# Transposing x on row halves into two banks, with fewer zero products and a newly written order of all engines

## The chip, the cores and the metric

The kernel runs on one core of a Trainium2 chip. The metric is the device time of one execution in microseconds; the time before, 137.42 us, is the median of three runs.

## The reference

Sliding-window attention with a linear position bias, and behind it a token-mixing layer whose weights are made from the attention's output. Eight batches, eight heads, 576 tokens, head dimension 64, so a model width of 512.

```python
scores = q @ k.T / sqrt(64) + slope[h] * -(i - j)    # only where 0 <= i - j < 128
attn   = softmax(scores);  x = attn @ v              # per batch and head
x      = x transposed to (batch, token, 512)
W_tok  = (x @ w_q) @ (x @ w_k).T / 8                 # 576 x 576 per batch
out    = relu(W_tok @ x) @ w_out
```

## The kernel before, in words

The work of a batch is cut into named steps, and everything that an engine does stands in one written table, `ORDER` (line 49). An entry such as `XT2.0:P00` gives the step, the engine (P TensorE, A ScalarE, D VectorE, G GpSimd's DMA queue, S SyncE's DMA queue) and for TensorE the PSUM pair and bank: there are four pairs of two banks, one digit names a whole pair, two digits one bank. `follow` (line 145) walks through the table and each step's instructions are issued in that order, so every engine's queue is exactly its column of the table, in order. Semaphores between engines are put in from the data.

The steps of batch b, key block or row block in the second number:
- `LF`, `Lq`, `Lk`, `Lv`, `Lt` load q, k, v and the 64 tail tokens. The first six, `LF`, bring batch 0's first blocks in fp32 through the queues of ScalarE and SyncE, 128 KB each (line 412). All others go through GpSimd's queue and are cast to fp16 on the way.
- `TF`, `TJ`, `TQ`, `TK`, `TT` transpose q and k on TensorE (lines 465 to 608), and `EF`, `EJ`, `ETQ`, `ETK`, `ETT` copy them from PSUM to `qkT`. TK uses the helper `tp2` (line 245): it transposes 64 rows at a time, the upper and the lower half into two different banks of a pair, so 16 small transposes make one step.
- `QK` makes the scores of four heads for 128 keys, `EXP` (line 657) exponentiates them on ScalarE into `pt`, and one `MUL` (line 672) on VectorE multiplies the eight heads of a key block by the tabled exponential of bias and mask.
- `PV` multiplies by v with a column of ones; `RC` takes the reciprocal of the sums and `X` (line 733) scales into `x`, 128 tokens at a time. Part 4 is the tail of 64 tokens.
- `XT` (line 749) transposes two blocks of x: eight transposes of 128 x 128 into one bank. `EXT` copies the result to `xT`. The other branch in the same function, for b >= `PAIRED`, does it with `tp2` into both banks of a pair, sixteen transposes of 64 rows; with `PAIRED = 9` and eight batches it is never taken. `XTT` does the tails.
- For a pair of batches (0 and 1, 2 and 3, ...; steps carry the even number) `WK`, `WQ`, `WT` project with w_k and w_q, `G` makes the 64 x 512 product of keys and x, `MX` the mixed tokens, `RM` and `RMT` the relu, `OUT` the output product of 128 tokens, `EO` the copy to one of 14 buffers `osb` and `DO` the store to memory, through SyncE's queue with two exceptions on ScalarE's.
- `WM` (line 297) issues products of a zeroed tile with itself, whose result nobody reads; `WARM` gives their number at each place of the table.

The work of a pair's mixing and output lies in the table among the scores of the next batches. Only the last pair's has nothing to lie beside.

Of the kernel before, what the change touches and what calls it, by code (L numbers as in the profile page):

```python
# [15 lines left out]
S = 576  # L16
D = 64
# [25 lines left out]
PAIRED = 9  # L43
# [7 lines left out]
zeros:D LF0.1.0.1:S Lv2.4:G ones.1:D Lq0.2:G pads:D Lk0.2:G wmc:D WM.0:P31 TF0.0.0:P00 Lk0.1:G  # L51
ones.3:D bias:A Lq1.0:G ones.0:D TF0.0.1:P01 idh:D Lk1.0:G TF0.1.1:P10 EF0.0.1:D Lk1.1:G
TF0.1.0:P11 EF0.1.1:D Lv0.0:G EF0.0.0:A EF0.1.0:A Lk1.2:G Lk1.3:G WM.1:P31 TJ0.2.1:P1
QK0.0.1:P0 QK0.0.0:P2 EJ0.2.1:D Lv0.1:G TJ0.2.0:P30 EXP0.0.0:A TJ0.1.1:P1 EJ0.2.0:D Lk0.3:G
EXP0.0.1:A QK0.2.1:P3 EJ0.1.1:D QK0.2.0:P2 QK0.1.1:P1 EXP0.2.1:A MUL0.0:D TQ1:P0 EXP0.2.0:A
Lv0.2:G QK0.1.0:P3 Lt0:G ETQ1:D EXP0.1.0:A TK1.0:P2 ETK1.0:D EXP0.1.1:A Lv1.0:G MUL0.2:D
WM.2:P01 QK1.1.1:P2 QK1.1.0:P3 QK1.0.1:P1 EXP1.1.1:A Lv1.1:G QK1.0.0:P0 MUL0.1:D EXP1.1.0:A
Lq2.0:G TK1.1:P2 ETK1.1:D EXP1.0.1:A Lk2.3:G PV0.0:P3 QK1.2.1:P2 RC0.0:D Lk2.2:G X0.0:D
EXP1.0.0:A PV0.1:P1 MUL1.1:D PV0.2:P3 Lv1.2:G EXP1.2.1:A QK1.2.0:P0 Lv0.3:G RC0.1:D EXP1.2.0:A
X0.1:D TT0:P2 RC0.2:D Lv1.3:G TJ0.3.1:P1 X0.2:D ETT0:A XT0.0:P00 ETT1:A MUL1.0:D Lk2.0:G  # L60
EJ0.3.1:A WM.3:P01 QK1.3.0:P2 Lv0.4:G EXP1.3.0:A EXT0.0:D PV1.0:P1 QK0.3.1:P3 RC1.0:D PV1.1:P0
X1.0:D EXP0.3.1:A QK0.3.0:P2 MUL1.2:D QK1.3.1:P1 EXP0.3.0:A TQ2:P3 Lk2.1:G RC1.1:D EXP1.3.1:A
MUL0.3:D Lv1.4:G ETQ2:A WM.4:P21 TK2.1:P1 X1.1:D Lt1:G ETK2.1:D PV1.2:P2 XT1.0:P00 RC1.2:D
PV0.3:P3 X1.2:D Lw1:G QK2.2.1:P1 MUL1.3:D Lk3.1:G EXP2.2.1:A Lw0:G RC0.3:D WM.5:P01 PV1.3:P2
EXT1.0:A X0.3:D Lq3.0:G PV0.4:P01 RC1.3:D X1.3:D TK2.0:P3 QK2.2.0:P1 Lv2.0:G RC0.4:D PV1.4:P00
ETK2.0:D EXP2.2.0:A XT1.1:P20 Lk3.0:G RC1.4:D X0.4:D QK2.0.0:P3 EXT1.1:D XT0.1:P21 EXP2.0.0:A
# [93 lines left out]
def kernel(  # L160
# [914 lines left out]
```

## Time and profile before

| | us |
|---|---|
| median of three runs | 137.42 |
| lowest and highest | 137.33, 138.28 |
| span of the profiled execution, first to last instruction | 135.4 |
| median less span | 2.0 |
| TensorE busy | 122.8 |
| VectorE busy | 114.0 |
| ScalarE busy | 107.3 |
| GpSimd busy (it issues the loads, 0.9 us each) | 86.3 |

The profiled execution's own time is known by its span of 135.4 us; the runs' times are taken around the whole execution, and their median lies 2.0 us above it. Times in views count from the start of the span. A row of a group gives line, engine, operation, destination and sources, shape and count, then the busy time of all, the mean of one in ns, and the idle time of the engine just ahead of them with what ended it. A row of the table of stretches gives the stretch and its length, then busy time (and count) of TensorE, its weight loads (PEld), VectorE, ScalarE and GpSimd, the granted clock, the DMA share and GB/s. Busy times of TensorE overlap, so its share reads high.

### The profile page before, as it was taken

Reading aid. Unit: us, or ns where it says so; the run is one execution under the profiler, and the core shown is the slowest. Engines: PE = TensorE matmul, PEld = TensorE weight load, DVE = VectorE, ACT = ScalarE, POOL = GpSimd, SP = SyncE. Lnnn points to the kernel's source line nnn. Section 1 sums busy time; section 2 is a strip of 40 time slices with the busy share of each in tenths; the row PEclk is TensorE's granted clock in tenths of the full one; section 3 lists DMA queues with packets and bytes.
Section 4 is the critical chain, followed back from the end, with each engine's and each line's share of the span. In section 5 each row is a group of like instructions: output and inputs, shape, how many; then the busy total and the mean of one; then the engine's idle time right before and its main releaser. Section 6 shows DMA issues by size and latency. Waiting matters only on the chain.

```text
span 135.4 us, 5054 instructions
## 1 busy us (share of the span) xinstructions
PE 122.8 (91%) x2174; PEld 78.1 (58%) x2174; DVE 114.0 (84%) x197; ACT 107.3 (79%) x145; POOL 86.3 (64%) x108
## 2 busy tenths in 40 slices
PE   6598867889999799999999999999999999999970
PEld 2264546666676476575566576565685576634440
DVE  5733899999999999998999999699999999557830
ACT  2574999995999999998999999999999962367040
POOL 7998979599979759899999999997000000000000
PEclk9999999999999999999999999999999999999999
DMA  4999999999999999999999999999999900858894
GB/s 106 211 165 169 155 156 180 165 158 154 167 159 163 195 184 153 157 154 157 155 157 158 152 153 155 151 185 258 269 223 348 331 14 5 258 185 328 264 368 151
DMA packets 105414, 24.97 MB, mean 184 GB/s; under 512 B 95536, under 2 KB 100912, under 8 KB 105392
## 3 DMA queue, kind: packets, MB, share of 16 engines
q0 software_dynamic: 96832, 14.42, 150.2%
q1 hardware_dynamic: 6688, 9.44, 20.4%
q10 hardware_dynamic: 1872, 0.79, 2.2%
q8 instruction: 17, 0.28, 0.8%
q14 instruction: 5, 0.04, 0.1%
HBM read 29.62 MB, written 9.44 MB: 288 GB/s over the span
## 4 chain that ended last, share of the span: by engine, by line
PE 67%; DVE 13%; ACT 10%; DMA 3%; issue 3%; ACTq 1%; DVEq 0%
PE pair L240 54%; PE pair L243 12%; ACT pt L657 6%; DVE pt L672 4%; DVE qkT L254 4%; DMA osb<-in_q_dram 3%; DVE x L733 3%; ACT qkT L252 2%; DVE rm L888 1%; ACTq L412 1%; ACT rm L886 1%; DVE inv L723 1%; ACT wqT L252 0%; DVE xT L254 0%; ACT gs L252 0%
## 5 line engine op out<-in xcount | busy, mean ns | idle before, releaser
L657 ACT ACTIVATE pt<-pair 128x1024 f16<-128x1024 f32 x64 | 62.8, 1038 | 6.5 <-PE pair L240 5.9
L672 DVE TENSOR_TENSOR pt<-pt,bias 128x2048 f16<-128x2048 f16 x32 | 38.5, 1217 | 0.4 <-ACT pt L657 0.3
L393 POOL DMA_DIRECT2D vt<-in_v_dram x40 | 35.3, 968 | 1.1 <-issue 0.5
L240 PE MATMUL pair<-wout_sb,rm 128*128 128x512 f16 (+1 forms) x132 | 31.7, 373 | 0.0
L367 POOL DMA_DIRECT2D natk<-in_k_dram x31 | 28.6, 947 | 2.9 <-DMA natq<-in_q_dram 1.6
L240 PE MATMUL pair<-vt,pt 128*128 128x65 f16 (+1 forms) x576 | 21.9, 194 | 1.9 <-DVE rm L888 0.5
L240 PEld LDWEIGHTS <-pt 128*128 128x128 f16 (+1 forms) x576 | 19.1, 100 | 7.6 <-issue 3.4
L240 PE MATMUL pair<-qkT 64*128 64x256 f16 (+2 forms) x320 | 22.3, 250 | 1.3 <-DVE qkT L254 0.8
L254 DVE COPY qkT<-pair 128x1024 f16<-128x1024 f16 (+2 forms) x27 | 19.3, 734 | 4.1 <-PE pair L243 3.9
L733 DVE TENSOR_TENSOR x<-pair,inv 128x512 f16<-128x512 f32 x32 | 21.8, 690 | 0.9
L252 ACT COPY osb<-pair 128x512 f32<-128x512 f32 (+1 forms) x24 | 14.0, 596 | 10.5 <-PE pair L240 9.7
L240 PEld LDWEIGHTS <-rm 128*128 128x128 f16 x132 | 11.4, 97 | 12.1 <-issue 2.2
L240 PEld LDWEIGHTS <-qkT 64*128 64x128 f16 x320 | 11.1, 94 | 8.6 <-issue 5.4
L254 DVE COPY osb<-pair 128x512 f32<-128x512 f32 (+1 forms) x13 | 8.7, 668 | 5.1 <-PE pair L240 5.1
L379 POOL DMA_DIRECT2D natq<-in_q_dram x12 | 11.5, 995 | 2.2 <-PE pair L240 1.6
L886 ACT ACTIVATE rm<-pair 128x1024 f16<-128x1024 f32 x11 | 11.1, 1045 | 0.5 <-PE pair L240 0.3
L243 PE MATMUL pair<-identh,x 128*128 128x128 f16 x128 | 9.8, 220 | 0.0
L240 PE MATMUL pair<-warm 128*128 128x512 f16 x22 | 7.8, 491 | 1.5 <-DVE warm L295 1.2
L243 PEld LDWEIGHTS <-x 128*128 128x128 f16 x128 | 7.6, 98 | 2.3 <-issue 1.2
L254 DVE COPY xT<-pair 128x1024 f16<-128x1024 f16 x11 | 7.5, 685 | 1.2 <-PE pair L243 1.1
L243 PE MATMUL pair<-identh,natk 64*128 64x64 f16 x248 | 6.5, 191 | 1.2 <-ACT pt L657 0.9
L243 PEld LDWEIGHTS <-natk 64*128 64x128 f16 x248 | 5.3, 94 | 3.9 <-issue 3.3
(68 smaller groups left out, 136.2 us busy)
## 6 DMA issues: line engine op xcount, KB each, us to landing
out_dram<-osb SPq DMA_DIRECT2D x30, 256.0 KB, 3.5
vt<-in_v_dram POOLq DMA_DIRECT2D x32, 128.0 KB, 7.2
natk<-in_k_dram POOLq DMA_DIRECT2D x31, 128.0 KB, 5.8
natq<-in_q_dram POOLq DMA_DIRECT2D x4, 512.0 KB, 7.7
natq<-in_q_dram POOLq DMA_DIRECT2D x12, 128.0 KB, 5.7
out_dram<-osb SPq DMA_DIRECT2D x9, 128.0 KB, 2.5
vt<-in_v_dram POOLq DMA_DIRECT2D x8, 64.0 KB, 5.7
natt<-in_q_dram POOLq DMA_DIRECT2D x4, 128.0 KB, 5.7
```

The lines of the kernel that those rows point to most:

```text
L240: hold(nc.tensor.matmul(*a, **k))
L243: hold(nc.tensor.transpose(*a))
L252: hold(nc.scalar.copy(out_ap, in_ap))
L254: hold(nc.vector.tensor_copy(out=out_ap, in_=in_ap))
L367: return lambda: nc.gpsimd.dma_start(out=natk(b, n), in_=k[b, :, P * n:P * n + P, :].transpose([1, 0, 2]))
L379: return lambda: nc.gpsimd.dma_start(out=rows_q(b)[:, r], in_=q[b, :, 0:512, :].rearrange("h (p r) d -> r p h d", r=QR)[r])
L393: return lambda: nc.gpsimd.dma_start(out=vtv(b, t)[:n, :, 0:D], in_=v[b, :, P * t:P * t + n, :].transpose([1, 0, 2]))
L412: (nc.scalar if o.eng == "ACT" else nc.sync).dma_start(out=nat32(j, n)[:, 4 * u:4 * u + 4, :], in_=(q, k)[j][0, 4 * u:4 * u + 4, P * n:P * ...
L657: nc.scalar.activation(out=pt, in_=two(hold_.bank).rearrange("p e c -> p (e c)"), func=AF.Exp, scale=SCALE)
L672: nc.vector.tensor_tensor(out=pv, in0=pv, in1=bt, op=ALU.mult)
L733: nc.vector.tensor_tensor(out=x_s[b % NX][qt].rearrange("p (g h d) -> p g h d", g=2, h=4), in0=sums(p)[:, :, :, 0:64], in1=box["inv"].unsq ...
L886: hold(nc.scalar.activation(out=out_ap, in_=in_ap, func=AF.Relu, scale=WSCALE))
```

## The change

`PAIRED` goes from 9 to 0: every XT now takes 64 rows at a time with `tp2`, the two halves into the two banks of a pair, and EXT reads both. `WARM` goes from 22 zero products at six places to 15 at four: seven ahead of everything, two ahead of the first scores, two between the first scores and the next, four in batch 1. `ORDER` is another table: the same steps (less two WM), but another order on every engine, other engines for many copies, and other banks.

```diff
-PAIRED = 9
+PAIRED = 0
...
-WARM = (6, 9, 1, 1, 2, 3,)
+WARM = (7, 2, 2, 4,)
...
 ORDER = """
-warm:D LF0.0.0.0:A LF0.0.1.0:S ones.2:D iota:G LF0.0.1.1:A LF0.1.0.0:S ident:G LF0.0.0.1:A
...
+warm:D iota:G ones.2:D LF0.0.1.0:S LF0.1.0.0:A WM.0:P31 ident:G LF0.0.0.0:S wmc:D LF0.1.0.1:S
+Lq0.2:G LF0.0.0.1:S Lk0.2:G ones.1:D LF0.0.1.1:S bias:A Lk0.1:G idh:D pads:D TF0.1.0:P00 ones.0:D
```

The engines' queues at three places. First ScalarE at the start of the program; `osb` are the first loads, `bias` the table of the mask, `qkT0` batch 0's transposed q and k, `pt` the exponentials, `pair` a PSUM pair. Before:

```order
L412 DMA osb_145<-in_q_dram 128x4x64
L412 DMA osb_147<-in_k_dram 128x4x64
L412 DMA osb_145<-in_q_dram 128x4x64
L336 ACT_TABLE_LOAD
L336 ACTIVATE bias_71<-wm_70 128x384 x8
L252 CAST qkT0_76<-pair0_140 128x2x2x128
L252 CAST qkT0_76<-pair1_141 128x2x128
L657 ACTIVATE pt0_98<-pair2_142 128x1024
```

Now:

```order
L408 DMA osb_151<-in_q_dram 128x4x64
L332 ACT_TABLE_LOAD
L332 ACTIVATE bias_71<-wm_70 128x384 x8
L248 CAST qkT0_76<-pair1_141 128x2x2x128
L248 CAST qkT0_76<-pair0_140 128x2x2x128
L248 CAST qkT0_76<-pair0_140 128x2x128
L653 ACTIVATE pt0_98<-pair1_141 128x1024
L248 COPY qkT0_76<-pair0_140 128x4x256
L653 ACTIVATE pt0_98<-pair1_141 128x1024
```

Two of its three loads have moved to SyncE's queue; it has one copy of transposed blocks more ahead of its first exponential, and another between the first and the second. (Lines of the changed kernel are four lower.)

SyncE's queue, where the first stores stand. Before, the first three rows behind the loads:

```order
L412 DMA osb_147<-in_k_dram 128x4x64
L412 DMA osb_154<-in_q_dram 128x4x64 x2
L993 DMA out_0_dram<-osb_2048 128x512
L993 DMA out_0_dram<-osb_1219 128x512
L993 DMA out_0_dram<-osb_2022 128x512
```

Now:

```order
L408 DMA osb_149<-in_k_dram 128x4x64
L408 DMA osb_164<-in_q_dram 128x4x64
L408 DMA osb_151<-in_q_dram 128x4x64
L408 DMA osb_164<-in_q_dram 128x4x64
L408 DMA osb_149<-in_k_dram 128x4x64
L989 DMA out_0_dram<-osb_1364 128x512
L989 DMA out_0_dram<-osb_1542 128x512
L989 DMA out_0_dram<-osb_1250 128x512
L992 DMA out_0_dram<-osb_1189 64x512 x2
```

The queue has five first loads where it had three. Its first store was DO3.3, which stands in the table behind the exponentials of batch 6's third block; now it is DO0.1, behind those of batch 3, and five more stores of batches 0 and 1 follow it among the steps of batch 4.

VectorE from its last multiply (`pt`) on; `inv` and `invt` are reciprocals, `x32` a block of x of batch 7, `xtl` tails, `xT` the copied transposes of x, `wqT` and `wkt` projections. Before:

```order
L672 TENSOR_TENSOR pt0_98<-pt0_98,bias_71 128x2048
L888 TENSOR_SCALAR rm0_136<-pair0_140 128x8x4x32
L254 CAST wqT1_129<-pair1_141 128x64
L254 CAST wkt1_133<-pair1_141 64x2x64 x2
L723 RECIPROCAL inv_2634<-pair3_143 128x8
L733 TENSOR_TENSOR x32_118<-pair3_143,inv_2634 128x512
L723 RECIPROCAL inv_2649<-pair2_142 128x8
L723 RECIPROCAL inv_2651<-pair1_141 128x8
L733 TENSOR_TENSOR x33_119<-pair2_142,inv_2649 128x512
L733 TENSOR_TENSOR x30_116<-pair1_141,inv_2651 128x512
L723 RECIPROCAL inv_2679<-pair3_143 128x8
L733 TENSOR_TENSOR x31_117<-pair3_143,inv_2679 128x512
```

Now, from the fifth row behind the last multiply on; ahead of these stand the reciprocals and products of two other blocks of batch 7:

```order
L719 RECIPROCAL inv_2702<-pair0_140 128x8
L729 TENSOR_TENSOR x33_119<-pair0_140,inv_2702 128x512
L719 RECIPROCAL inv_2740<-pair3_143 128x8
L729 TENSOR_TENSOR x23_115<-pair3_143,inv_2740 128x512
L716 RECIPROCAL invt_2792<-pair0_140 128x4
L723 TENSOR_TENSOR xtl1_121<-pair0_140,invt_2792 128x256
L716 RECIPROCAL invt_2812<-pair0_140 128x4
L723 TENSOR_TENSOR xtl1_121<-pair0_140,invt_2812 128x256
L250 COPY xT2_124<-pair3_143 128x2x4x2x64
L250 COPY xTt1_127<-pair1_141 128x512
L250 CAST gs1_135<-pair1_141 128x512
```

A relu and, behind the rows shown, six copies of the output of batches 4 and 5 have left the end of VectorE's queue; blocks of batch 6 that stood ahead of the last multiply (x23 and the tails) now stand behind it, and the copies of xT follow them directly. In TensorE's queue, behind the last scores, 14 output products stand where 19 stood (a product of halves counted as one), and WT6 stands behind WK6, where it stood ahead of the last PV steps.

More of the change, by code (lines that the diff above doesn't have):

```diff
@@ L55 @@
[L55 to L60, printed above, removed]
@@ L115 @@
-OUT6.2:P11 DO7.2:A EO6.0:D OUT6.1:P30 DO6.0:S EO6.2:D OUT6.3:P10 DO6.2:S EO6.1:D OUT7.0:P11
-DO6.1:S EO6.3:D OUT7.1:P30 DO6.3:S EO7.0:A OUT7.3b:P10 DO7.0:S EO7.1:A OUT7.3a:P11 EO7.3b:D
-DO7.1:S DO7.3b:A EO7.3a:A DO7.3a:S
+warm:D iota:G ones.2:D LF0.0.1.0:S LF0.1.0.0:A WM.0:P31 ident:G LF0.0.0.0:S wmc:D LF0.1.0.1:S
+Lq0.2:G LF0.0.0.1:S Lk0.2:G ones.1:D LF0.0.1.1:S bias:A Lk0.1:G idh:D pads:D TF0.1.0:P00 ones.0:D
+Lt0:G TF0.0.0:P01 zeros:D TF0.1.1:P10 TF0.0.1:P11 EF0.1.1:D Lk0.3:G ones.3:D WM.1:P31 Lq1.0:G
```

119 lines of the change are left out of this document (61 added, 58 removed).

## The prediction

> **What bounds the kernel now.** I read the slices of the page first, then the table of stretches, the groups by shape, the order of events at both ends, and the landings of loads.
>
> Busy tenths of TensorE (PE), VectorE (DVE) and ScalarE (ACT) in 40 slices of 3.4 us:
>
> ```profile
> span 135.4 us, 5054 instructions
> PE   6598867889999799999999999999999999999970
> DVE  5733899999999999998999999699999999557830
> ACT  2574999995999999998999999999999962367040
> ```
>
> All three engines are nearly full from slice 6 to slice 32; then two of them thin out and TensorE alone stays full to slice 39. So there are three different stages. The table of stretches (length, then busy time and count of each engine) is cut at the first bias multiply (13.99), the 9th exponential (19.41), the 57th (94.30), the end of the last multiply (109.03), the projections of the last pair (116.28) and the end of TensorE (131.32):
>
> ```profile
> 13.99:19.41 5.42, 3.90 (x90) 2.71 (x86) 5.36 (x6) 5.42 (x6) 4.82 (x6) 1.00 2.42 156
> 19.41:94.30 74.89, 71.29 (x1481) 48.06 (x1481) 71.70 (x118) 70.42 (x92) 68.75 (x81) 1.00 2.22 166
> 94.30:109.03 14.73, 14.70 (x303) 9.44 (x300) 14.43 (x24) 14.48 (x24) 0.00 (x0) 1.00 1.35 280
> 109.03:116.28 7.25, 7.25 (x105) 4.74 (x99) 6.78 (x15) 2.90 (x4) 0.00 (x0) 1.00 0.12 43
> 116.28:131.32 15.04, 15.04 (x121) 7.29 (x119) 8.97 (x13) 6.28 (x9) 0.00 (x0) 1.00 0.82 282
> 131.32:135.40 4.08, 0.00 (x1) 0.00 (x0) 0.03 (x1) 0.37 (x1) 0.00 (x0) 1.00 0.56 182
> ```
>
> From the first multiply to the end of the last, 95.04 us, VectorE is busy 5.36 + 71.70 + 14.43 = 91.49 and idle 3.55; ScalarE is idle 4.72, TensorE 5.15. Nothing in that stretch can shrink by much unless VectorE is given less. Behind it, TensorE is the only bound.
>
> **The change, part by part.** The groups by shape (count, then busy time in all and mean ns of one) give the prices:
>
> ```profile
> L672 DVE TENSOR_TENSOR pt<-pt,bias 128x2048 f16<-128x2048 f16 x32 | 38.5, 1217 | 0.4 <-ACT pt L657 0.3
> L243 PE MATMUL pair<-identh,x 128*128 128x128 f16 x128 | 9.8, 220 | 0.0
> L243 PE MATMUL pair<-identh,natk 64*128 64x64 f16 x248 | 6.5, 191 | 1.2 <-ACT pt L657 0.9 <-DVE x L733 0.3
> L254 DVE COPY xT<-pair 128x1024 f16<-128x1024 f16 x11 | 7.5, 685 | 1.2 <-PE pair L243 1.1
> L252 ACT COPY xT<-pair 128x1024 f16<-128x1024 f16 x5 | 5.1, 1026 | 0.0
> L254 DVE COPY qkT<-pair 128x1024 f16<-128x1024 f16 x14 | 9.5, 684 | 0.8 <-PE pair L243 0.7
> L254 DVE COPY qkT<-pair 128x2048 f16<-128x2048 f16 x6 | 7.3, 1220 | 0.2
> L888 DVE TENSOR_SCALAR rm<-pair 128x1024 f16<-128x1024 f32 x5 | 6.0, 1217 | 0.0
> L254 DVE COPY osb<-pair 128x512 f32<-128x512 f32 x12 | 8.3, 688 | 3.6 <-PE pair L240 3.6
> L254 DVE COPY qkT<-pair 128x512 f16<-128x512 f16 x7 | 2.8, 418 | 3.1 <-PE pair L243 3.1
> L727 DVE TENSOR_TENSOR xtl<-pair,invt 128x256 f16<-128x256 f32 x8 | 3.4, 419 | 0.2
> L720 DVE RECIPROCAL invt<-pair 128x4 f32<-128x4 f32 x8 | 1.4, 176 | 0.4 <-PE pair L240 0.2
> ```
>
> *Transposes of x on halves.* Sixteen XT steps take 9.8 us, 0.61 each. The key transposes already have the new form: 248 / 16 = 15.5 groups in 6.5 us, 0.42 each. TensorE saves 16 x 0.19 = 3.1 us. The copy behind it costs what it did: qkT, read from two banks, 684 ns, xT from one 685. By itself that is worth nothing, since VectorE holds the stretch.
>
> *VectorE from first to last multiply.* Counted in the two order tables, the new stretch has fewer of: ETQ one (1.22), ETK two (1.37), EXT four (2.74), reciprocal and product of the tail rows two (2 x 0.60 = 1.19), in all -6.5. It has more of: three ETT, one EJ, one EXTT (5 x 0.42 = 2.1), copies EG two, EWQ, EWK, EO two (6 x 0.69 = 4.1), EWT one in three parts (0.8, from ScalarE's and VectorE's small casts, an estimate), RM two (2.43), in all +9.4. Net +2.9; five instructions more overlap their neighbours by 0.08 each (two multiplies in a row start 1.13 apart, not 1.22), so +2.5. Nothing hides it: it lies on the engine that holds the stretch.
>
> *ScalarE and TensorE there.* From its first to its last exponential ScalarE gets three EXT (1.03), one ETQ and two ETK, one RM, one RMT and two EO more, and loses three ETT, two EG, EWK, EWQ, EWT and EXTT: +4.2 by the same kinds of rows. But before, 3.6 us of copies ran between the last exponential and the end of the last multiply; now 1.0 does. So the stretch gets +1.6, against 4.72 idle and the 2.5 by which it grows; if that cover failed whole, it would cost 1.6. TensorE gets five output products (0.86 each, 36 matmuls in 7.08 below: 4.3), and its XT steps there are twelve of 0.42 where they were fourteen of 0.61 (-3.5), WT6 leaves it (-0.5): +0.3 against 5.15 idle. That is where the saved 3.1 goes: it pays for the products.
>
> *From the last multiply to the end.* The order of events, before:
>
> ```profile
> 107.81 1.22 DVE L672 TENSOR_TENSOR pt<-pt,bias 128x2048 f16<-128x2048 f16 x1
> 113.34 0.69 DVE L733 TENSOR_TENSOR x<-pair,inv 128x512 f16<-128x512 f32 x1
> 114.79 1.02 ACT L252 COPY xT<-pair 128x1024 f16<-128x1024 f16 x1
> 118.19 1.03 PE L240 MATMUL pair<-x,wk 128*64 128x512 f16 x8
> 124.24 7.08 PE L240 MATMUL pair<-wout_sb,rm 128*128 128x512 f16 x36
> 132.24 0.33 SPq L961 DMA_DIRECT2D out_dram<-osb  x1
> ```
>
> Before, 7.25 us pass from the last multiply to WK6, filled with five older output products. Now VectorE has behind the last multiply: four times reciprocal and x (start to start 0.85), two of the tail (0.54), one EXT (0.61), so 5.1, and WK6 follows it: -2.1. From WK6 on, three older products before G6 and the Relus' end become one: -2 x 0.9; WT6 comes in, +0.5; and since only OUT4.1 and OUT7.4 (1.7) lie against EG6 and the four Relus, which take 0.7 + 2.5 on two engines, TensorE waits some 0.5. Net -0.8 on 15.04. The last 4.08 stays. In all -2.9.
>
> *The head.* Before:
>
> ```profile
> 1.25 1.04 SPq L412 DMA_DIRECT2D osb<-in_q_dram  x2
> DMA to landing us min/median/max: 2.6/3.2/4.6
> 6.56 2.02 PE L243 MATMUL pair<-ident,osb 128*128 128x128 f32 x8 [1.65 <-DMA osb<-in_q_dram]
> 8.40 2.92 PE L240 MATMUL pair<-warm 128*128 128x512 f16 x9
> 9.66 0.15 PEld L240 LDWEIGHTS <-warm 128*128 128x128 f16 x1 [0.28 <-issue]
> 10.08 0.75 PEld L240 LDWEIGHTS <-warm 128*128 128x128 f16 x4 [0.27 <-issue]
> 11.38 0.60 PE L240 MATMUL pair<-qkT 64*128 64x256 f16 x8
> 12.02 10.26 ACT L657 ACTIVATE pt<-pair 128x1024 f16<-128x1024 f32 x11 [2.75 <-PE pair L240]
> 13.99 1.23 DVE L672 TENSOR_TENSOR pt<-pt,bias 128x2048 f16<-128x2048 f16 x1 [0.33 <-ACT pt L657]
> ```
>
> The transposes end at 8.58, but nine zero products hold the first scores until 11.38. Now two remain there. Five of the six first loads go through SP's queue, 0.52 apart, so the last is issued at 2.8 and lands at 6.0 to 7.4, about when the last one does now; one third of the transposes is then left. The first scores come near 8, two exponentials and one copy later the first multiply, near 11.1, 2.9 earlier. That is not all kept: the second multiply needs exponentials whose scores now stand behind TT0 and its load, Lq1.0 is issued two loads later than it was, and VectorE idles between its first two multiplies. Followed through to ETK1.0 (the first copy that batch 1's scores need), I find it ready 1.4 earlier with every load on time. Bounds: 0 and 2.9; I take 1.2, near the followed one.
>
> *Clock.* In the rows above the zero products start 0.42 apart up to 10.08 and 0.19 apart behind it: TensorE ran at half rate until then, though the granted clock reads 1.00. [...] It gives no other sum, only the second rival.
>
> *Loads and stores.* POOL's loads of 64 to 128 KB land so, in 57 to 80 us and in 85 to 97 us, with seven stores issued from 88.11:
>
> ```profile
> DMA to landing us min/median/max: 5.3/5.7/5.8
> DMA to landing us min/median/max: 5.1/9.6/10.2
> 88.11 6.10 SPq L993 DMA_DIRECT2D out_dram<-osb  x7
> ```
>
> The new order issues six stores around 56 to 65, among the loads. Seven stores cost the loads 10.2 - 5.7 = 4.5, so six up to 3.9. By counting VectorE's work ahead of each use and 0.87 us per load ahead of each issue, the keys of TK6.0 and TK5.1 have 1 to 3 us to spare there. Bounds 0 and 3.9; I take 0, the lower one, because these stores follow their copies one by one, over some 9 us, where the seven had piled up.
>
> **Sum** against the span: -1.2 + 2.5 - 2.9 = -1.6, so 133.8 for 135.4. The median of the runs is 2.0 above this span (137.42), and I keep that distance: 135.8.
>
> **Rivals.**
> 1. *More of the head is kept.* The full 2.9 makes the sum -3.3, and 0.6 less idle on VectorE, as TensorE has saved work, makes 133.5. For it: the rows of the zero products; against: the loads of the head.
> 2. *The half rate stays through the first scores.* TensorE's 4.7 us of work up to the 9th exponential doubles in part; 1.5 of it (two scores, TQ1, TK1.0) lies on the path, the gain at the head is gone: 137.3. For: fifteen zero products, not 22.
> 3. *The stores hold up the loads.* TK6.0, TT4 or TK5.1 stand in TensorE's queue ahead of scores; waiting 2 us there stops all three engines: 137.8. It begins where landings come later than the 1 to 3 us to spare.
> 4. *Two banks are too many (slower).* An XT step and its copy now hold a whole pair of banks for some 0.25 + 0.69 us where one bank was held and the other free for a product. TensorE's queue is in order, so a step that finds no pair stops all behind it. Price: 0.25 each, sixteen times, 4.0, so 139.8; it turns slower by over 1% from 0.19 each, 3.0 in all. For: three engines with 4 to 5 us idle in 95; against: the key steps already take pairs, with few waits. [...]
> 5. *The change to halves does nothing visible*: part of the forecast, as VectorE holds the stretch.
>
> **Numbers.** Chances: forecast 0.45 (own range 134.2 to 137.2), rivals 1 to 4: 0.10, 0.15, 0.15, 0.15. A measurement of this kernel can tell about 1% (1.4 us) from no change. Faster: 0.10 and 0.37 of the forecast's 0.45; within 1%: 0.08, 0.15 and 0.08 of rival 3; slower: 0.07 of rival 3 and 0.15. That is 0.47, 0.31, 0.22. The range 133.4 to 139.0 leaves out the upper half of rival 4 and a little below.
>
> **What would show it.** Right: first multiply at 11 to 12.5, last multiply ending near 110, WK6 5 us behind it, TensorE's end 14 us behind that; XT steps of 0.4 us; VectorE idle about 3.5 in between. Wrong: scores at half rate (spacing 0.2 instead of 0.1), TensorE waiting for natk or natt near 64 to 72, or for copies ahead of XT steps. If VectorE is idle much over 5 us between its multiplies, the forecast fails.

## The result: 5.5% slower

| | before | after |
|---|---|---|
| median of four runs each, same chip | 137.78 us | 145.13 us |
| range | 137.33 to 138.28 | 144.84 to 146.59 |
| ratio, 95% interval | | 1.0548, 1.0497 to 1.0598 |
| profiled execution: time, span | span 135.4 | 145.2, span 143.3 |

The forecast was 135.8, with a range of 133.4 to 139.0. The span grew by 7.9 us, where -1.6 was expected. (The profiled runs of twice_early, vector_less and old_fill, below, were slower than the others of the same kernel; places and waits are read from them, not times; medians below are of all runs, ratios leave such runs out.)

### The profile after

First the page, in the order used for the kernel before: the span, the busy tenths of TensorE, VectorE and ScalarE in slices of 3.6 us, and the granted clock.

```profile
span 143.3 us, 5292 instructions
PE   6789679788886879999989999999999999898960
DVE  6424487999887879998889999999898999425110
ACT  4847968867995989999899999999998888458540
PEclk9965855999999999999999999999999999999997
```

Of the first 14 slices (50 us) TensorE stays under 9 in twelve and VectorE in eleven, and the clock row has 5s and 8s up to 25 us, where before every stretch read 1.00. (The views count time without a clock record as full; the records begin at 10.06 before and at 4.92 after, so the 1.00 that the prediction read beside slow products ahead of 10.06 is no measurement.) The table of stretches, cut at the same events (first multiply, 9th and 57th exponential, end of the last multiply, WK6, end of TensorE):

```profile
13.32:22.01 8.69, 6.24 (x117) 4.86 (x118) 6.40 (x8) 5.71 (x6) 6.12 (x9) 0.70 2.31 160
22.01:104.37 82.36, 75.40 (x1668) 51.04 (x1664) 74.78 (x125) 74.70 (x93) 67.63 (x80) 0.98 2.11 165
104.37:118.00 13.63, 13.11 (x163) 7.11 (x160) 13.22 (x19) 12.68 (x17) 0.00 (x0) 1.00 0.64 224
118.00:123.73 5.73, 4.92 (x144) 3.55 (x142) 4.77 (x14) 3.66 (x5) 0.00 (x0) 1.00 0.85 277
123.73:139.30 15.57, 14.09 (x142) 7.12 (x136) 4.86 (x6) 9.15 (x18) 0.00 (x0) 1.00 0.53 177
```

The first three rows are the stretch from first to last multiply: 8.69 + 82.36 + 13.63 = 104.68 us for 95.04. VectorE is busy for 6.40 + 74.78 + 13.22 = 94.40 of them (91.49 before) and idle for 10.28 (3.55 before). By the prediction's three terms:

| term | predicted | measured in the profiled runs |
|---|---|---|
| first multiply earlier | -1.2 (kept of 2.9) | 13.99 to 13.32: -0.67 |
| first to end of last multiply | +2.5, idle unchanged | +9.64: busy +2.9, idle +6.7 |
| last multiply to end of span | -2.9 | 26.37 to 25.30: -1.07 |

So VectorE's work was counted right, and nearly the whole error is idle time that was taken as unchanged. Of the idle time 6.3 us lie ahead of 50 us, where before had 0.8. The events of the head, in order of time:

```profile
7.79 1.13 PE L239 MATMUL pair<-ident,osb 128*128 128x128 f32 x4 [0.65 <-DMA osb<-in_q_dram]
13.32 1.23 DVE L668 TENSOR_TENSOR pt<-pt,bias 128x2048 f16<-128x2048 f16 x1 [0.27 <-ACT pt L653]
13.78 1.47 PE L236 MATMUL pair<-qkT 64*128 64x256 f16 x12
14.44 3.77 ACT L653 ACTIVATE pt<-pair 128x1024 f16<-128x1024 f32 x4 [1.16 <-PE pair L236]
16.41 1.23 DVE L668 TENSOR_TENSOR pt<-pt,bias 128x2048 f16<-128x2048 f16 x1 [1.87 <-ACT pt L653]
```

Two things are to be seen. The last transposes of the first loads begin at 7.79 after a wait for a load; before, all were done at 8.58. And twelve score products take 1.47 us, 0.42 per step of four, where before eight took 0.60 (0.22 per step of four). At that pace ScalarE waits 1.16 for scores and VectorE 1.87 for exponentials.

Behind 30 us stands something that the trace of before had not shown as costly. TensorE stops in the middle of a step, and no engine is named as what ended the stop:

```profile
37.61 0.30 PE L239 MATMUL pair<-identh,natk 64*128 64x64 f16 x9 [0.54 <-issue]
44.08 0.38 PE L236 MATMUL pair<-wqk_sb,xTt 128*64 128x64 f16 x13 [1.33 <-issue]
122.36 0.24 PE L239 MATMUL pair<-identh,x 64*128 64x64 f16 x5 [0.81 <-issue]
```

These are the middles of TK2.1, WT0 and XT6.1. In the trace's list of DMA packets there is a queue of instructions, 18 packets of 16384 bytes on queue 8 in all (17 before), and TensorE's records fit them. The three stops, and a smaller one at 50.28, lie whole multiples of 256 records (products and weight loads together) apart, and each ends 1.35 to 1.52 us after a packet has ended:

```
stop ends   records since the last stop   packet on queue 8      resumed after it by
 37.61                 -                  35.33 to  36.22        1.39
 44.08                256                 41.66 to  42.56        1.52
 50.28                256                 47.88 to  48.83        1.45
122.36             11 x 256               118.96 to 121.01       1.35
```

So 256 records are called a block here. The counts agree with it: 4590 records and 18 packets after, 4348 and 17 before, 255 and 256 to a packet. The packets at 41.66 and 47.88 start 4.05 and 3.80 us after the block before began, and end 0.90 and 0.95 later; the blocks that begin at 31.86, 37.61 and 44.08 lasted 5.75, 6.47 and 6.20 us, the stops behind them included. That TensorE had used up a block and waited for the packet with the next is the reading of these times; no record ties a packet to a block. Stops of this kind (block ends at which neither a product nor a weight load runs, 1.2 to 1.7 us behind a packet) add up to 3.3 us after, and to none before, where the ends can be counted from the stops of old_twice_inst below. The longest takes 1.33 us in one place.

The transposes of x themselves did what was said of them:

```profile
L239 PE MATMUL pair<-identh,x 64*128 64x64 f16 x256 | 6.3, 191 | 1.0 <-issue 0.8
```

### The profile page after: what moved, and what is told of

Its sections match the earlier page's. It is cut to its first block, busy times and chain, and to the rows that moved or that the text cites. A ratio compares the mean times of both kernels' runs of the same rounds, so it can differ in the third digit from the quotient of the medians.

```text
span 143.3 us, 5292 instructions
## 1 busy us (share of the span) xinstructions
PE 124.1 (87%) x2295; PEld 78.7 (55%) x2295; DVE 109.5 (76%) x191; ACT 114.9 (80%) x151; POOL 86.4 (60%) x108
## 4 chain that ended last, share of the span: by engine, by line
PE 63%; DVE 14%; ACT 10%; issue 5%; DMA 4%; SPq 1%; DVEq 0%; ACTq 0%
PE pair L236 52%; PE pair L239 11%; ACT pt L653 6%; DVE pt L668 5%; DMA osb<-in_q_dram 4%; DVE qkT L250 3%; DVE x L729 3%; ACT rm L882 2%; DVE inv L719 1%; SPq L408 1%; DVE rm L884 1%; ACT rmt L882 1%; ACT osb L248 1%; DVE xtl L723 0%; ACT wk L248 0%
## 5 line engine op out<-in xcount | busy, mean ns | idle before, releaser
L236 PE MATMUL pair<-qkT 64*128 64x256 f16 (+2 forms) x320 | 25.6, 273 | 2.2 <-DVE qkT L250 1.3
L250 DVE COPY qkT<-pair 128x512 f16<-128x512 f16 (+2 forms) x27 | 17.7, 677 | 9.5 <-PE pair L239 9.3
L248 ACT COPY osb<-pair 128x512 f32<-128x512 f32 (+1 forms) x32 | 17.4, 589 | 6.9 <-PE pair L236 6.2
L236 PEld LDWEIGHTS <-qkT 64*128 64x128 f16 x320 | 12.5, 101 | 11.0 <-issue 6.1
L248 ACT COPY xT<-pair 128x1024 f16<-128x1024 f16 x9 | 9.0, 1012 | 1.3 <-PE pair L239 0.9
L882 ACT ACTIVATE rm<-pair 128x1024 f16<-128x1024 f32 x9 | 9.1, 1036 | 0.5 <-PE pair L236 0.5
L884 DVE TENSOR_SCALAR rm<-pair 128x1024 f16<-128x1024 f32 x7 | 8.3, 1216 | 0.7 <-PE pair L236 0.7
L248 ACT COPY qkT<-pair 128x1024 f16<-128x1024 f16 (+1 forms) x6 | 7.8, 1306 | 1.2 <-PE pair L239 1.2
L239 PEld LDWEIGHTS <-natq 128*64 128x64 f16 (+2 forms) x256 | 6.5, 109 | 3.5 <-issue 3.3
L239 PE MATMUL pair<-identh,natq 128*64 128x128 f16 (+2 forms) x256 | 7.5, 211 | 1.0 <-ACT pt L653 0.6
```

The lines of the kernel that those rows point to most:

```text
L236: hold(nc.tensor.matmul(*a, **k))
L239: hold(nc.tensor.transpose(*a))
L248: hold(nc.scalar.copy(out_ap, in_ap))
L250: hold(nc.vector.tensor_copy(out=out_ap, in_=in_ap))
L882: hold(nc.scalar.activation(out=out_ap, in_=in_ap, func=AF.Relu, scale=WSCALE))
L884: hold(nc.vector.tensor_scalar(out=out_ap, in0=in_ap, scalar1=0.0, scalar2=WSCALE, op0=ALU.max, op1=ALU.mult))
```

## The experiments

Theory: two costs in time that TensorE loses by itself, half rate ahead of 25 us and late instruction blocks behind 36, start most of VectorE's new idle time; late first loads are a smaller third. (The expectation of zero_fill still puts the clock down as a small part.) Rivals: only one of them; the pairs that XT holds; the early stores; VectorE's added work; the order as such. Ratios are to runs of the kernel before on the same chip, with 95% intervals; the forecast's bound of about 1% tells what counts as a difference.

| kernel | built on | median us | ratio | interval |
|---|---|---|---|---|
| zero_fill | after | 141.80 | 1.0286 | 1.0229 to 1.0343 |
| whole_x | after | 143.89 | 1.0396 | 1.0329 to 1.0463 |
| whole_x_pair | after | 144.02 | 1.0466 | 1.0422 to 1.0510 |
| shift_only | after | 143.17 | 1.0402 | 1.0346 to 1.0458 |
| late_stores | after | 145.71 | 1.0550 | 1.0463 to 1.0637 |
| fill_whole | after | 142.21 | 1.0314 | 1.0255 to 1.0372 |
| fill_two_queues | after | 141.10 | 1.0210 | 1.0131 to 1.0289 |
| two_queues_whole | after | 140.88 | 1.0225 | 1.0172 to 1.0277 |
| vector_less | after | 142.69 | 1.0277 | 1.0202 to 1.0352 |
| vector_less_out | after | 141.26 | 1.0218 | 1.0154 to 1.0283 |
| old_twice_inst | before | 140.65 | 1.0226 | 1.0172 to 1.0281 |
| twice_early | before | 139.86 | 1.0130 | 1.0061 to 1.0199 |
| twice_late | before | 138.15 | 1.0051 | 1.0015 to 1.0086 |
| old_few_zero | before | 137.21 | 0.9953 | 0.9905 to 1.0001 |
| old_head | before | 139.01 | 1.0056 | 1.0012 to 1.0100 |
| old_fill | before | 138.19 | 1.0043 | 0.9995 to 1.0090 |
| old_vector_more | before | 139.47 | 1.0079 | 1.0032 to 1.0126 |

### The holes filled: zero_fill

```diff
-WARM = (7, 2, 2, 4,)
+WARM = (7, 2, 2, 4, 2, 1, 2, 2, 2,)
-TF0.0.0:P01 ... TF0.1.1:P10 ... TT0:P0 ... QK0.2.1:P1 ... QK0.1.0:P3 ... TJ0.3.1:P1
+TF0.0.0:P01 WM.4:P31 ... TF0.1.1:P10 WM.5:P31 ... QK0.2.1:P1 WM.6:P00 ... QK0.1.0:P3 WM.7:P00 ... TJ0.3.1:P1 WM.8:P00 TT0:P0
```

> The changed kernel with nine zero products more in its sparse head: two and one between the first fp32 transposes, and two each ahead of QK0.1.0, TJ0.3.1 and TT0, which is moved behind TJ0.3.1, so that pair 0 stands free for them. Theory (instruction blocks and late first loads; the clock is a small part): 144.0 to 145.5, the granted clock near 1.00 and TensorE's stalls at the ends of its 256-instruction blocks still there. Rival (the half rate up to 25 us starts all of VectorE's idle time before 50 us): VectorE's idle of 1.87 ahead of MUL0.2 and 0.93 ahead of ETK1.1 goes, the first 9 exponentials end 2 earlier: 142 or less.

141.8: 3.3 us less for nine products that nobody reads. The scores and the first two multiplies:

```profile
12.77 0.87 PE L236 MATMUL pair<-qkT 64*128 64x256 f16 x12 [0.20 <-DVE qkT L250]
13.22 1.23 DVE L668 TENSOR_TENSOR pt<-pt,bias 128x2048 f16<-128x2048 f16 x1 [0.51 <-ACT pt L653]
15.17 1.23 DVE L668 TENSOR_TENSOR pt<-pt,bias 128x2048 f16<-128x2048 f16 x1 [0.72 <-ACT pt L653]
```

Twelve products now take 0.87 us, the wait of 1.87 is 0.72, and the 9th exponential starts at 20.03 for 22.01. So the rival was right on the time and the theory, which had put the clock down as a small part, was wrong on it. It is not all clock: 1.3 us of the gain lie behind the last multiply, which ends at 116.08 with 24.0 us to the end of the span instead of 25.3. Eighteen more instructions have moved the ends of the blocks by nine products. One still lies inside XT6.1, at 119.28, but its packet (116.14 to 117.38) is there in time; and late_stores below, with the TensorE instructions of after, passes its own without a stop too (124.41, packet until 123.00). So these 1.3 us go with when a packet comes, and that the holes have a part in it is not shown. The largest stop is still there, 1.73 us at 41.15.

### The ends of blocks moved alone: shift_only

```diff
+            for _ in range(9 if i == 0 else 0):
+                mm(one(o.bank)[:, 0:32], warm[:, 0:P], warm[:, 0:32], start=True, stop=True)
```

> The changed kernel with nine more zero products, as in the kernel with filled holes, but of 32 columns and all at the start, where TensorE waits for loads: the instruction blocks end at the same work as there, the holes stay open. That kernel gained 3.3 us. Theory (1.9 of it the full rate up to 20 us, the rest that the block that ended inside XT6.1 and the one inside TK2.1 end elsewhere): 143.3 to 144.6, first nine exponentials as in the changed kernel, end of the last multiply to end of span 24.0 to 24.6 instead of 25.3. Rival (all of it is the clock): 144.8 to 145.4. Rival (all is the blocks): 142.3 or less.

143.2, outside all three by a little, and it did not take the causes apart: nine products of 32 columns at the start were enough for the full rate (scores 0.22 apart from 12.93 on), so the 9th exponential came 2.0 earlier here too. What it adds is what became of these 2.0: at the end of the last multiply 0.75 are left (117.25 for 118.00). In between stands a block's end with a longer stop:

```profile
41.71 0.41 PE L236 MATMUL pair<-xT,wqk_sb 128*64 128x512 f16 x2 [1.94 <-issue]
```

The work ahead of it was ready sooner here, and the stop is longer, 1.94 instead of 1.33. Yet this is not where the gain goes: the 25th exponential, behind that stop, is 1.67 earlier than after (46.39 for 48.06), as the 17th was (1.64). It goes between the 25th and the 57th (103.62 for 104.37), where another stop, at 99.18, takes 0.74 instead of 0.14. The tail is 24.0, as with the filled holes.

### x transposed whole in the new order: whole_x and whole_x_pair

```diff
-PAIRED = 0
+PAIRED = 9
-XT0.0:P0 ...
+XT0.0:P00 ...
```

The second kernel keeps `banks=2` for each XT and writes one of the two.

> The changed kernel with PAIRED = 9: x transposed whole, eight 128 x 128 products into one bank, the order of all engines kept. TensorE gets 256 instructions fewer and 16 x 0.19 = 3.0 us more work. Theory (blocks of 256 instructions that arrive later than they are used up): the stalls that start at 37.6, 44.1, 50.3 and 122.4 shrink from 2.9 to under 1.2, the work given back is covered before 110: 143.0 to 144.5. First rival (halves are a gain that this order needs): 146.5 to 148. Second rival (pairs held by XT are what stops TensorE, 0.25 each): 141 or less.

> As the kernel with x transposed whole in the new order, but each XT still holds both banks of its pair, of which it writes one. Theory (instruction blocks): as that kernel within 0.5, 143.0 to 144.5. Rival (banks): 1 to 4 slower than that kernel.

143.9 and 144.0, as the theory has it. Holding a pair costs nothing that can be told: the ratios differ by 0.7%, with an interval of about -0.1 to 1.5%. So rival 4 of the prediction, two banks too many at 4.0 us, falls, though a cost below some 2 us is not excluded. With 256 instructions fewer the stops sum to 1.3 and 1.1 us for 3.3, while the XT steps take 0.6 again. This holds over the study: the five traces of the new order with halves stop for 2.4 to 4.1 us at block ends, the six with x whole for 0 to 1.4. The halves save TensorE 3 us of products, and the kernel is 0.8 to 1.5% slower for them.

### More instructions in the old order: old_twice_inst, twice_early, twice_late

```diff
-                        tp(oneh(o.bank)[:, 256 * c + P * n:256 * c + P * n + P], x, identh)
+                        for r in range(2):
+                            tp(oneh(o.bank)[64 * r:64 * r + 64, 256 * c + P * n:256 * c + P * n + P],
+                               x[:, 64 * r:64 * r + 64], identh)
```

> The kernel before, its order and banks kept, with each 128 x 128 transpose of x cut into two of 64 columns that write the two halves of the same bank's partitions: twice as many instructions (256 more on TensorE) for the same data and one bank. Theory (instruction blocks): one more packet of instructions, stalls of 0.3 to 1.5 us at the ends of blocks between 30 and 52 us, so 138.5 to 140. Rival (the number of instructions costs nothing that can be seen): 137.0 to 138.0.

> The kernel before with the transposes of x cut in two only in batches 0 to 3: 128 instructions more on TensorE, used up between 23 and 63 us, while the loads run. With all 256 the time rose by 3.1. Theory (a packet of instructions is fetched 3 to 4 us after the block before it began while loads run, and 1 to 2 us after it where they don't): most of the cost is here, +1.5 to +3, 139.2 to 141. Rival (the cost is the instructions themselves, 0.012 us each): +1.5 here and as much in the other half.

> The kernel before with the transposes of x cut in two only in batches 4 to 7: 128 instructions more, used up between 75 and 116 us, where the loads thin out and end at 94. Theory: no stall at a block's end there, 0 to +0.7, 137.5 to 138.5. Rival: +1.5 as in the other half, 139.3.

Cutting the transposes in two changes neither order, banks nor data, and TensorE's busy time for them hardly:

```profile
L243 PE MATMUL pair<-identh,x 128*64 128x128 f16 x256 | 10.2, 222 | 0.0
```

That is 10.2 us for 9.8, and yet 3.1 us (2.3%) more in all. Stops of that kernel and of the one with the early half alone:

```profile
38.63 0.28 PE L240 MATMUL pair<-qkT 64*128 64x192 f16 x4 [0.32 <-issue]
45.10 0.39 PE L240 MATMUL pair<-qkT 64*128 64x256 f16 x4 [1.14 <-DVE qkT L254]
```

```profile
41.49 0.28 PE L240 MATMUL pair<-qkT 64*128 64x192 f16 x4 [2.01 <-issue]
```

All three resume 1.37 to 1.41 us after a packet's end. The second row shows how a releaser can mislead: the profile names a copy that ended just then, but before, the same scores (QK3.0.0) ran at 43.53, ahead of that copy; the stop is 256 records behind the first one. The stops of old_twice_inst come to 1.8 us in all, less than the 3.1. A second cost follows the long ones: the clock records read half rate from 47.17 to 50.58 behind the stop of 1.14, and from 43.18 to 46.60 behind that of 2.01.

Counted from these stops, the kernel before passes all its block ends without one. It does stop for 0.50 at 46.17, but that lies 35 records ahead of an end and waits for a relu on VectorE; the same product waits as long in five other kernels of the old order.

The early half of the instructions costs 1.3% (interval 0.6 to 2.0), the late half 0.5% (0.2 to 0.9), with no stop at a block's end in its profile. The intervals overlap, so the times alone do not part the halves; but the late one excludes the 1.5 us (1.1%) of the rival. In the traces it is not the instructions that cost but where they crowd: behind 75 us the blocks of twice_late last 4.8 to 7.9 us, and in the shortest of them (78.62 to 83.46) the next packet came 1.3 us after the start; at the stops between 30 and 52 us it came 3.0 to 4.7 after (3.47, 4.05 and 3.80 in after).

### Both cures: fill_whole

The edits of zero_fill and whole_x together, and four more products behind TK1.0.

> The changed kernel with both: the nine zero products of the kernel with filled holes and four more between TK1.0 and QK1.0.0 (where TensorE waited 1.07 us and fell to half rate again behind it), and x transposed whole in one bank. Alone the first took 3.3 us off and the second some 1.5. Theory (two separate costs: half rate ahead of 25 us, blocks of 256 instructions behind 36): they add up, 139.0 to 140.8, with score spacing of 0.22 up to 26 us and stalls at block ends under 1 us in all. Rival (both only shift the same waits): 141.2 to 142.5.

142.2, no less than the filled holes alone: the theory's sum fails. The stop at 41.7 fell from 1.73 to 0.35, as expected, and the 25th exponential came 0.45 earlier although the first was 0.6 later. But at the end of the last multiply nothing is left (116.45 for 116.08). TensorE's three microseconds are back, which may be why; no run shows it alone.

### The first loads on two queues: fill_two_queues, two_queues_whole

```diff
-LF0.0.0.1:S ... LF0.0.1.1:S
+LF0.0.0.1:A ... LF0.0.1.1:A
```

Both have the thirteen zero products; the second has x whole as well.

> The changed kernel with the same thirteen zero products (halves kept), and two of the five first loads, LF0.0.0.1 and LF0.0.1.1, moved from SyncE's queue to ScalarE's, where the kernel before has them. Theory (the queue makes the first operands late: five landed 3.58 to 8.22, ScalarE's one at 3.87): the last lands near 6.5, first exponential near 9, the time 139.5 to 141.0. Rival (the loads behind them set the head: natural-order q and k of batch 0 and 1): first exponential earlier but the 9th not, 141.0 to 142.3.

> The changed kernel with all three: thirteen zero products, two of the first loads back on ScalarE's queue, x transposed whole. With halves it took 141.1, stalled 1.65 us at the block's end at 39.3 and ran the products of WQ0 and WK0 at half rate behind it. Theory (that stall gives back what the head had gained): without it 139.0 to 140.4, the 25th exponential near 44.0. Rival (the natural-order loads, 0.87 us each, hold the stretch from 20 to 45): the 25th exponential again at 45.4 or later, 140.8 to 142.

141.1 and 140.9. The first exponential comes at 8.77 and 9.39, 1.0 to 1.6 earlier than after. With halves, the 25th is no earlier than without the edit (45.78 for 45.84): the gain ends at a stop. It is no longer than without the edit (1.65 for 1.73), but TensorE comes out of it at half rate, by the clock records from 39.38 to 42.79:

```profile
39.29 0.27 PE L239 MATMUL pair<-identh,natq 128*64 128x128 f16 x2 [1.65 <-issue]
39.34 1.92 PE L236 MATMUL pair<-xT,wqk_sb 128*64 128x512 f16 x8
```

WQ0's eight products take 1.92 us where after they took 1.03. With x whole the 25th exponential is at 44.05, level with before (43.96). This is the best of the new order, with all scores 0.22 apart. Its stretches, cut at the first multiply, the 25th exponential, the end of the last multiply and WK6, and those of before at the same events:

```profile
12.31:44.05 31.74, 26.98 (x606) 19.42 (x602) 28.58 (x46) 27.18 (x32) 26.25 (x32) 1.00 2.14 167
44.05:114.30 70.25, 68.07 (x1247) 43.41 (x1246) 66.12 (x106) 66.13 (x83) 48.54 (x57) 1.00 1.93 181
114.30:119.40 5.10, 5.10 (x112) 4.01 (x110) 4.68 (x14) 3.66 (x5) 0.00 (x0) 1.00 1.04 382
```

```profile
13.99:43.96 29.97, 26.38 (x616) 19.17 (x611) 29.22 (x46) 27.84 (x35) 26.22 (x32) 1.00 2.22 162
43.96:109.03 65.07, 63.52 (x1256) 41.05 (x1256) 62.27 (x101) 62.48 (x86) 47.35 (x56) 1.00 2.04 193
```

The first multiply is 1.7 earlier than before, the 9th exponential level already (19.47 for 19.41), and the 25th still. Behind it 70.25 us stand against 65.07, with VectorE 3.85, ScalarE 3.65 and TensorE 4.55 busier. The tail, 138.2 - 114.3 = 23.9, is 2.5 shorter than before, close to the 2.9 predicted. The kernel after at the same events:

```profile
13.32:48.06 34.74, 27.68 (x633) 20.93 (x633) 28.50 (x46) 27.18 (x32) 28.11 (x35) 0.88 2.09 170
48.06:118.00 69.94, 67.07 (x1311) 42.08 (x1310) 65.91 (x106) 65.92 (x84) 45.64 (x54) 1.00 1.86 174
```

So half of what it loses between the multiplies, 4.77 of 9.64 us, lies ahead of the 25th exponential, with VectorE idle for 6.24 where before had 0.75; here it is 3.16. The other half, 4.87, lies behind it, with each of the three engines 3.4 to 3.7 busier, and nothing that was tried touches it: that stretch takes 69.9 to 71.1 us in after and seven of the kernels built on it, and 71.2 to 73.9 in late_stores, vector_less and vector_less_out.

### The stores: late_stores

`DO3.1` ahead of the six early stores, and `OSB` from 14 to 19.

> The changed kernel with the six early stores (seven transfers) held behind DO3.1, so that they issue at some 92 instead of 64 to 74 us, with 19 instead of 14 output buffers so that no copy waits for them. Theory (the stores delay loads by some 5 us each, but the loads had that much to spare): 144.5 to 145.6. Rival 3 of the prediction (late keys stop the scores): 143.3 or less.

145.7, the same as after. Landings of the loads in 64 to 80 us, after and then here:

```profile
vt<-in_v_dram POOLq DMA_DIRECT2D x8, 128.0 KB, 8.9
natk<-in_k_dram POOLq DMA_DIRECT2D x3, 128.0 KB, 10.2
```

```profile
vt<-in_v_dram POOLq DMA_DIRECT2D x8, 128.0 KB, 5.3
natk<-in_k_dram POOLq DMA_DIRECT2D x3, 128.0 KB, 5.3
```

The stores do cost the loads 3.6 to 4.9 us each, and nobody waits for it: the 49th exponential is at 91.64 for 91.60. The stores held back then crowd into 92 to 103 us, where this kernel stops for 1.94 us at a block's end (102.03), which may hide a small gain.

### The head alone in the old order: old_few_zero, old_head, old_fill

```diff
-WARM = (6, 9, 1, 1, 2, 3,)
+WARM = (6, 2, 1, 1, 2, 3,)
```

`old_head` also moves Lv2.4 and Lv0.0 back in the queue of loads; `old_fill` has four more zero products ahead of TK1.1 instead. The gate of the expectations stands for the step from half to full rate, seen in before at 10.08, where the zero products start 0.42 us apart ahead of it and 0.21 to 0.22 behind it (the prediction has 0.19). That it takes nine of them was an assumption.

> The kernel before with two zero products instead of nine ahead of its first scores, nothing else changed. Theory (nine zero products open the gate): scores 0.42 apart instead of 0.22 up to some 17 us; the first exponential comes 1 to 2.5 earlier, but the 9th at the same time or later, so 137.3 to 139.5. Rival, the prediction's reading of the head (they only stand in the way): the first multiply 2 earlier, 135.3 to 136.6.

> The kernel before with two zero products instead of nine ahead of its first scores, and two moves in the queue of loads: Lv2.4 from the first place to behind Lv2.3, Lv0.0 from ahead of Lk1.2 to behind Lk1.3, so that the keys of TK1.1 are issued 1.7 earlier. With the zero products alone out, the first multiply came 2 earlier and TK1.1 waited 1.0 for those keys, fell to half rate, and by the 17th exponential all was given back. Theory (that load is what gives it back): 135.3 to 136.6. Rival (something else is late next, or the gate): 136.8 to 137.6.

> The kernel before with two zero products instead of nine ahead of its first scores, and four more ahead of TK1.1, where TensorE waited 1.0 us for keys and dropped to half rate behind it. Theory (that drop gave the head's 2 us back): 135.3 to 136.6. Rival (the loads hold the stretch behind it): 136.8 to 137.6.

137.2, 139.0 and 138.2: no gain that can be told from none. The rival was right about the first of them at its start: two zero products do, and its scores run at full rate (eight products in 0.62 us; before, 0.60). Its stretches, cut at the first multiply, the 9th and the 17th exponential and the end of the last multiply:

```profile
12.05:17.48 5.43, 3.78 (x82) 2.50 (x77) 5.31 (x5) 5.43 (x7) 4.49 (x6) 1.00 2.43 156
17.48:31.35 13.87, 11.45 (x240) 9.06 (x241) 11.88 (x20) 10.98 (x13) 11.33 (x14) 0.88 2.23 163
31.35:109.12 77.77, 75.73 (x1550) 49.72 (x1550) 74.44 (x122) 74.00 (x101) 59.07 (x70) 1.00 2.05 187
```

1.94 earlier at the first multiply and at the 9th exponential (17.48 for 19.41), 0.16 earlier at the 17th (31.35 for 31.51), 0.09 later at the last multiply. One trace says little about a head, though: in five profiled kernels that have the head of before unchanged the first multiply comes at 13.05 to 15.01 and the 9th exponential at 18.47 to 20.43. (In the four with the head of after the 9th comes at 22.01 to 22.26.) In the middle row TensorE waited for keys:

```profile
18.01 0.29 PE L243 MATMUL pair<-identh,natk 64*128 64x64 f16 x8 [0.99 <-DMA natk<-in_k_dram]
```

and ran at half rate behind that wait (clock 0.88). Loads moved forward, `old_head`, or products put into the wait, `old_fill`, did not keep the gain: in the profiled runs of both the first scores came at half rate (0.41 per step). So the head is held by several things in turn, and which one comes first differs between kernels that differ by a few products.

### VectorE's added work: vector_less, vector_less_out, old_vector_more

The first two give five copies and three copies of two_queues_whole back from VectorE to ScalarE (`EO1.2:D` to `EO1.2:A` and so on); the third gives five output copies of the kernel before to VectorE.

> The kernel with zero products, two queues and whole transposes (140.9), with five copies given back from VectorE to ScalarE: EO1.2, EWQ2, EG2, RM2.3 and EO3.0 (4 x 0.69 + 1.22 = 4.0 us off VectorE, some 3.4 onto ScalarE, which is idle for 8.7 of its 102 us between first and last multiply). Theory (what is left of the loss is VectorE's added work, 2.9 predicted and 3.2 measured in the busy times): 137.5 to 139.3. Rival (waits set that stretch, and VectorE only idles more): 140.0 to 141.5.

> The kernel with zero products, two queues and whole transposes (140.9) with three output copies, EO1.2, EO3.0 and EO4.2, given back from VectorE to ScalarE, which no later step of a batch waits for (3 x 0.69 = 2.1 less on VectorE, 1.8 more on ScalarE). Giving back five that included EWQ2, EG2 and RM2.3 made it slower, with ScalarE busy for 10.65 of 10.82 us between 63 and 74. Theory (VectorE's added work is part of what is left, and only the place of those five was bad): 138.8 to 140.0. Rival (the waits of this order take whatever is given): 140.4 to 141.5.

> The kernel before with five output copies between 57 and 72 us (EO1.3, EO1.1, EO1.2, EO1.0, EO1.4) moved from ScalarE to VectorE: 5 x 0.69 = 3.4 us more on VectorE, 3.0 less on ScalarE. Theory (as the prediction has it: VectorE holds the stretch, what is added there is paid in full): 140.2 to 141.2. Rival (the three engines hold it in turn, a part goes into waits that are there anyway): 138 to 139.5.

142.7 and 141.3, not faster than 140.9: the theory fell twice. (The two traces stop for 1.4 and 1.0 us at block ends near 40 and 47 us, ahead of the copies that were moved, where two_queues_whole had no stop; some of what was given back may hide there.) With five copies ScalarE is full where they went,

```profile
63.03:73.85 10.82, 9.45 (x183) 5.70 (x180) 6.54 (x10) 10.65 (x16) 10.08 (x12) 1.00 2.08 212
```

and VectorE idles there. In the old order 3.4 us more on VectorE, and 3.0 less on ScalarE, cost 1.1 us (0.8%, interval 0.3 to 1.3), about a third. So VectorE does not hold that stretch alone.

## Why the prediction was wrong

**VectorE, first to last multiply.** The step that failed. Its work was counted right (+2.9 counted and measured), but its idle time was kept at what it had been ("VectorE idle about 3.5 in between"), and that was wrong by 6.7 us: 5.5 of them ahead of the 25th exponential, 1.2 behind it. Of the 5.5, 3.1 come back once TensorE runs at full rate, the first loads come on two queues and x is transposed whole (two_queues_whole); that is what the runs show in place of an idle time that stays. The forecast also had too little for the other two engines in that stretch: ScalarE +1.6, measured +2.8; TensorE +0.3, measured +4.9, half rate included. "Nothing hides it" is neither shown nor refuted for this kernel: behind the 25th exponential 3.6 us more work goes with 4.9 us more time, while in the old order, where ScalarE was relieved, a third of added work was paid.

**Half rate.** Rival 2 named the place and gave it 0.15 and 137.3, with 1.5 us on the path. The mechanism was right and its size too small: with the holes filled the 9th exponential comes 2.0 earlier, and 1.9 of it are left at the last multiply. (The rest of the 3.3 is the stop in XT6.1.) The prediction read the nine zero products as what held up the scores; old_few_zero shows that this was true, and that they could go, but not in an order whose head has holes. The clock records of after, from 4.92 to 25.40, are 3.41 and 6.83 us long; the views in lengths of 3.41 from 8.39 on:

```profile
8.39:11.80 3.41, 3.29 (x45) 1.88 (x46) 0.00 (x0) 2.80 (x5) 3.41 (x5) 0.50 2.37 158
11.80:15.22 3.42, 3.42 (x49) 1.94 (x45) 1.98 (x3) 2.27 (x3) 2.22 (x3) 0.51 1.73 185
15.22:18.63 3.41, 1.80 (x46) 1.49 (x44) 2.22 (x5) 2.99 (x4) 2.65 (x3) 0.99 2.42 157
18.63:22.05 3.42, 2.58 (x44) 2.09 (x45) 2.96 (x4) 1.98 (x3) 2.81 (x4) 0.50 2.42 154
22.05:25.46 3.41, 3.14 (x52) 2.33 (x48) 2.49 (x4) 3.41 (x4) 3.41 (x5) 0.51 2.17 164
25.46:28.87 3.41, 2.35 (x58) 1.92 (x53) 3.38 (x6) 2.94 (x4) 3.09 (x4) 1.00 1.89 178
```

The window busy for 3.42 us (second number) is followed by full rate; the one that was busy for 1.80 of 3.41, with no hole above 0.62 us, by half rate. How busy a window is does not decide it alone: at half rate the window busy for 3.14 us was followed by full rate and the one busy for 3.29 by half. Of the full-rate windows up to 28.87 the two that half rate followed were busy for 1.76 (4.98 to 8.39) and 1.80, the one that it did not follow for 2.35. What in a window sets the rate of the next is not shown.

**Instruction blocks.** Missing from the prediction, in the sum and in the rivals. The 256 instructions that the halves add were priced at their saving in busy time only. That the saving "pays for the products" leaves out the stops, which grew by 3.3 us; old_twice_inst shows that 256 such instructions cost 3.1 us in the old order, where nothing else changed. How much of the loss they are in the new order is not shown: once the holes are filled, x whole, with hardly a stop, is no faster than halves.

**The head.** 1.2 were to be kept; 0.67 came at the first multiply, which is less than executions of one head differ by, and nothing was kept behind it. The estimate "6.0 to 7.4" for the last of five loads on one queue was too early: the last two landed at 7.74 and 8.22. Even with loads and clock put right the 9th and 25th exponentials are level with before, and with the shorter head in the old order the 17th is. The right term was 0.

**The tail.** -2.9 was predicted, -1.07 measured. In the ten other kernels of the new order, none of which stops there, it is -1.7 to -2.8: the step was nearly right, and much of the difference goes with the stop in XT6.1.

**Halves, stores, banks.** That the halves do "nothing visible" (rival 5) holds only with the holes filled, where whole or halves make no difference; with the holes open the halves are slower. Rival 3 had the delay of the loads about right (up to 3.9 expected, 3.6 to 4.9 measured) and the consequence wrong. Rival 4 at its price is excluded by whole_x_pair.

**What stays open.** Of the 7.4 us lost, 4.2 come back with zero products, queues and whole transposes together. What is left lies behind the 25th exponential, between 44 and 114 us: 5.2 us more than before there, against some 2.4 won in the head and the tail together. By the price of old_vector_more VectorE's 3.85 would be about 1 of it, but all three engines have more to do there, so that price may be too low; which engine or wait holds the stretch no run here says. How the gain of the filled holes divides between rate and blocks is also only bounded, since shift_only changed both; and why the packet for XT6.1 came late after and in time elsewhere is open. No kernel of the study beat both by more than the measurement can tell; the nearest is old_few_zero.

## What to carry to other kernels

Count an engine's instructions as well as its busy time: where 256 of TensorE's records took 5.75 to 6.47 us with the stop behind them (31.86 to 50.28 us, after), the stops were 0.26 to 1.33 us, and a step that swaps one product for two smaller ones can lose. Before taking zero products out or thinning a head, add up TensorE's busy time window by window of 3.4 us: in after the full-rate windows that half rate followed were busy for 1.76 and 1.80 us of 3.41, the one that it did not follow for 2.35. And follow a gain to the next common event, as the 25th exponential here: in one trace each, old_few_zero was 1.9 us ahead at the 9th and level at the 17th, fill_two_queues 1.2 ahead of zero_fill at the 9th and level at the 25th.

## What the runs showed of the hardware

- The row of the granted clock can read full while TensorE runs at half rate, because time without a clock record counts as full. whole_x's records begin at 20.40 us; its row reads 9 up to the last slice, and its scores stand 0.42 apart in the head all the same. The first records of before, at 10.06, and of after, at 4.92, are of full rate. From whole_x:

```profile
13.78 1.47 PE L236 MATMUL pair<-qkT 64*128 64x256 f16 x12
```

```profile
PEclk9999999999999999999999999999999999999996
```

  The start to start of like products is the better clock in the head: 0.42 apart there, 0.22 in zero_fill.
- Behind some stops at block ends TensorE ran at half rate: WQ0 behind the stop of 1.65 us took 1.92 instead of 1.03 (fill_two_queues, after), and the records read half rate for 3.41 us behind stops of 1.14 (old_twice_inst), 1.94 (late_stores) and 2.01 (twice_early) as well; behind those of 1.33 (after), 1.73 (zero_fill) and 1.94 (shift_only) they do not.
- A packet of instructions took 0.88 to 0.97 us in 14 of 18 places of after, and 2.05 among the last stores (at 118.96); work that had stopped resumed 1.35 to 1.52 after a packet's end (after), and 1.37 to 1.41 (old_twice_inst, twice_early).
- With seven stores among the loads the median landing of loads of v and k was 8.9 and 10.2 us (after), without them 5.3 (late_stores).
